# Moving the second batch's probability transposes from TensorE to VectorE and DMA

## The chip, the cores and the metric

One core of a Trainium2 chip runs the whole program. The metric is the device time of one execution in microseconds (us). The kernel was timed three times: median 715.22 us, lowest 714.57, highest 715.26.

## The reference

Causal attention of 4 batches, 12 heads, 448 positions and head size 64, and behind it a gated MLP over the 1,792 tokens (768 features, 1,536 hidden). Cut to what matters:

```python
scores = np.matmul(q, k.transpose(0, 1, 3, 2)) / np.sqrt(64)
scores = np.where(mask, -1e9, scores)            # mask: key later than query
attn = np.exp(scores - scores.max(-1, keepdims=True))
attn = attn / (attn.sum(-1, keepdims=True) + 1e-9)
x = np.matmul(attn, v)                            # then heads side by side: (1792, 768)
gate = 1.0 / (1.0 + np.exp(-(x @ w_gate)))
out = (gate * (x @ w_val)) @ w_out
```

The MLP's weights arrive as 8-byte numbers.

## The kernel before

**Units.** A batch is a unit. Its attention is done in six pairs of heads (`HP = 6`; pair `n` is `batch * 6 + k`), its MLP in 36 weight blocks of 128 by 768. Attention of batch 0 runs first by itself. Then the MLP of unit u runs on TensorE interleaved with the attention of batch u+1, u = 0 to 3; unit 3 has no attention beside it.

**MLP (L566 to L635).** Every product is made of three matmuls of 448 columns (high by high, high by low, low by high part), so a block is 18 matmuls on one stationary block of 128 by 128 each. `weight(p)` (L531) brings the block. In unit 0 each of the 36 blocks is loaded as 8-byte numbers into a part of the buffer `room` (L542, ring of three parts), ScalarE takes the high words (L545), three VectorE instructions assemble a 4-byte number (L547, L549, L552; tile `wr`, ring of three), and SyncE stores it to `wdram` (L555) for the later units, which only load it (L557). ScalarE then makes the high part `wh` (L560) and GpSimd the low part `wl` (L561), rings of three. So VectorE converts weights in unit 0 alone.

**Attention, narrow path (batches 0 and 1, `b < WIDE`).** Query blocks of 112 rows. `score` (L250): matmuls into the PSUM tiles `s`. `softmax` (L271): VectorE masks and takes the extreme (L279), ScalarE exponentiates (L283), VectorE adds 1e-9 and inverts once a pair (L290, L291), GpSimd scales (L302). `trans` (L304): 20 TensorE transposes in five groups into the PSUM tile `t`, each group emptied into `pt` by ScalarE or VectorE (L324, L326); `EV[1]` gives all five groups of batch 1 to ScalarE. `pv` (L328): 16 matmuls with `v` as the stationary operand and `pt` as the moving one. `features` (L345) splits the result into `xh` (ScalarE) and `xl` (VectorE).

**Attention, wide path (batches 2 and 3).** Query blocks of 128 rows, the last of 64 rows with both heads in one block. `wscore` (L366) and `wsoftmax` (L386) do the same work in other shapes (L396, L402), but add and invert three times a pair (L410, L412) and scale at L417. `shift` (L423) replaces the TensorE transposes: eight VectorE 32x32 transposes (L434, L437) write a buffer of 128 by 2048 named `tb`, and 16 DMAs of 64 KB (L443) issued by SyncE move its sixteen blocks of 32 partitions to their places in `pt`. `tb` is one of two halves of a stretch of `room`, which unit 0's weight loads use before. `wpv` (L447) makes 40 matmuls of 128 or 64 columns out of it.

**Order.** Nothing is ordered by hand. Each operation goes to `Plan.op` (L92) with its engine, a cost estimate, what it reads and writes, and sometimes a due time; a buffer that is used again waits for all operations of its former holder. `Plan.order` (L137) plays a list schedule: the engine that can start first takes, among its ready operations, the one with the earliest due time. The start times of that play fix the order of instructions on each engine, SyncE's queue of DMAs included, and each engine works strictly in that order:

```python
t = max(free[e], min(o.ready for o in q))
...
o = min((o for o in q if o.ready <= t + LOOK), key=lambda o: (o.due, o.n))
```

`att_steps` (L485) cuts a batch's attention into steps: at step m, scores of pair m, transposes of pair m-1, product with v of pair m-2 (`LAG = 1`). The main loop (L643) lets a step in each time its share of the attention falls behind the share of the MLP done, with the MLP's share divided by 0.9 in unit 0 and 0.98 later. A step of the wide path counts 1.0, one of the narrow path its estimated TensorE time.

Of the kernel before, what the change touches and what calls it, by code (L numbers as in the profile page):

```python
# [8 lines left out]
F32 = mybir.dt.float32  # L9
# [17 lines left out]
HP = H // 2  # L27

LAG = 1
WIDE = 2  # L30
WC = 512
EV = ((2,), (0, 1, 2, 3, 4), (1, 3, 4), (1, 3, 4))
BUFS = dict(w64=3, wd=2, wr=3, ws=3, sm=4, raw=3, pt=3, gt=5, vr=2, st=3)
LAT, LOOK, SLACK = 0.17, 0.06, 0.2


# [147 lines left out]
def kernel(  # L184
# [11 lines left out]
    def new(tag, shape, dtype, bufs=1, space=None):  # L196
        if tag not in pools:
            kw = {"space": space} if space else {}
            pools[tag] = ctx.enter_context(tc.tile_pool(name=tag, bufs=bufs, **kw))
        return plan.buf(pools[tag], bufs, shape, dtype, tag)  # L200
# [11 lines left out]

    room = new("room", [128, BUFS["w64"] * 2 * DM], F32)
    parts = []

    def part(n, k, i, both=False):

        old = parts[-BUFS["w64"]:] if both else parts[-k:-k + 1 or None]
        p = Part(room, i % k * n, n, Gone(old))
        parts.append(p)  # L220
        return p
# [17 lines left out]
    def load(n):  # L239
        j = pairs[n]  # L240
        j["raw"] = r = new("raw", [128, 2 * S], F32, BUFS["raw"])
        plan.op("SP", dma(128 * 2 * S * 4), lambda: nc.sync.dma_start(out=r.t, in_=qkt[n]), writes=[(r,)], extra=2.0)

    def load_v(n):
        j = pairs[n]
        j["vr"] = v = new("vr", [128, NB, 2, D], F32, BUFS["vr"])
        plan.op("SP", dma(128 * NB * 2 * D * 4), lambda: nc.sync.dma_start(
            out=v.t.rearrange("p c z d -> p (c z d)"), in_=vt[n]), writes=[(v,)], extra=2.0)

    def score(n, blocks, due):  # L250

        j = pairs[n]
        if blocks[0] == 0:
            j["sm"] = [new("sm", [128, SMW], F32, BUFS["sm"]) for z in range(2)]
            for k in ("mn", "sum", "r"):
                j[k] = new(k, [128, 2, NB], F32, BUFS["st"])
        r = j["raw"]
# [163 lines left out]
    shifted = []  # L421

    def shift(n):  # L423

        j = pairs[n]
        j["pt"] = pt = new("pt", [128, PTW], F32, BUFS["pt"])
        tb = part(4 * WC, 2, n, not shifted)
        shifted.append(tb)
        tv = lambda: tb.t.rearrange("p (r n) -> p r n", r=4)
        plan.op("PL", 0.2, lambda: nc.gpsimd.memset(tv()[:, 2:4, WC - 32:WC], 0.0), [], [(tb, "zero")])  # L430
        for z, i in [(z, i) for i in range(3) for z in range(2)] + [(0, 3)]:
            sm, o, c, at = j["sm"][z], woff(i), min(i + 1, 3), z * 192 + ioff(i) if i < 3 else 384
            r = [(sm, (i, z))] if i < 3 else [(sm, (i, 0), (i, 1))]
            plan.op("DVE", dve(128 * c) + 0.1, lambda sm=sm, i=i, o=o, c=c, at=at: nc.vector.transpose(  # L434
                out=tv()[:, :, at:at + 32 * c].rearrange("p r (c j) -> p c r j", j=32),
                in_=sm.t[:, o:o + 128 * c].rearrange("p (c r j) -> p c r j", r=4, j=32)), r, [(tb, (z, i))])
        plan.op("DVE", 0.2, lambda sm=j["sm"][0]: nc.vector.transpose(  # L437
            out=tv()[:, 0:2, WC - 32:WC],
            in_=sm.t[:, woff(3) + 384:woff(3) + 448].rearrange("p (r j) -> p r j", j=32)),
            [(j["sm"][0], (3, 0), (3, 1))], [(tb, "end")])  # L440
        for a in range(4):
            for r in range(4):
                plan.op("SP", 0.64, lambda a=a, r=r: nc.sync.dma_start(  # L443
                    out=pt.t[32 * r:32 * r + 32, a * WC:a * WC + WC], in_=tv()[32 * a:32 * a + 32, r]),
                    [(tb, "zero", "end", *[(z, i) for z in range(2) for i in range(3)], (0, 3))], [(pt, (a, r))], extra=2.0)
# [39 lines left out]
    def att_steps(b):  # L485

        L = []
        for m in range(HP + LAG + 1):
# [3 lines left out]
            if c is not None:  # L492
                L.append((0, lambda due, c=c: load_v(c)))
            if b >= WIDE:
                if c is not None:
                    L.append((0, lambda due, c=c: shift(c)))
                one, two = [], []
                if n is not None:
                    for bl, tag in ((0, 1), "s"), ((2,), "t"):
                        one.append((sum(keys(i) / 600 for i in bl) + 0.2, lambda due, n=n, bl=bl, tag=tag: wscore(n, bl, tag, due)))  # L500
                if d is not None:
                    two.append((2.0, lambda due, d=d: wpv(d, due)))
                if n is not None:
                    two.append((0.9, lambda due, n=n: wscore(n, (3,), "s", due)))
                for mine in (one, two):
                    if mine:
                        L.append((sum(w for w, _ in mine), lambda due, mine=mine: together(due, *(f for _, f in mine)), 1.0))
                    else:
                        L.append((0, lambda due: None, 1.0))
                continue  # L510
# [162 lines left out]
def _lay(q, k, v, moe_w_gate, moe_w_val, moe_w_out):  # L673
# [4 lines left out]
    vp = v.reshape(B * HP, 2, S, D)  # L678
    m = WIDE * HP
    vt[:m, :QB] = vp[:m].reshape(m, 2, NB, QB, D).transpose(0, 3, 2, 1, 4)  # L680
# [36 lines left out]
```

## Time and profile before

| | before |
|---|---|
| three timed runs, median (lowest to highest) | 715.22 us (714.57 to 715.26) |
| the profiled execution's own time | 714.69 us |
| its span, first to last instruction | 713.0 us |
| TensorE matmul busy | 688.6 us (97%) |
| VectorE busy | 315.3 us (44%) |
| ScalarE busy | 334.4 us (47%) |
| GpSimd busy | 435.0 us (61%) |
| mean granted TensorE clock | 0.988 of full speed |

The execution took 1.7 us more than its span. Busy time is the union of an engine's instruction times; matmuls are pipelined, so a busy TensorE is not one at its peak. The shares are means over stages that differ much: the first 66 us are the attention of batch 0, up to 258 us is unit 0 with the attention of batch 1, up to 418 us unit 1 with batch 2, up to 580 us unit 2 with batch 3, and then unit 3 by itself.

### The profile page before, as it was taken

What the parts mean: (1) busy time and instruction counts of PE and PEld (TensorE: products, weight loads), DVE (VectorE), ACT (ScalarE), POOL (GpSimd) and SP (SyncE); (2) the same over time, 40 slices, a digit from 0 to 9 for tenths busy, and PEclk for the clock granted to TensorE, in tenths of its full rate; (3) what the DMA queues carried; (4) which work ended last, traced back from release to release, by engine and by line L of the source; (5) the groups of instructions that cost most, each with busy time, mean ns of one, the idle gap of its engine ahead of it and who ended that gap; (6) DMA issues with size and microseconds to landing.
All of it is one profiled execution on the core that took longest, in us unless ns stands there. A gap on an engine that the chain in (4) does not pass through costs nothing.

```text
span 713.0 us, 11056 instructions
## 1 busy us (share of the span) xinstructions
PE 688.6 (97%) x3888; PEld 576.6 (81%) x3888; DVE 315.3 (44%) x784; ACT 334.4 (47%) x721; POOL 435.0 (61%) x388
## 2 busy tenths in 40 slices
PE   7989989899899899999999999999999999999997
PEld 4546767668688788888889988888889999999997
DVE  4898997788985324444541024444541000100000
ACT  6775546575565345543542245544552233333321
POOL 3472684858767456677665456677665456666652
PEclk9998999999899999999999999999999999999999
DMA  5484676676668435555466535555555433333341
GB/s 182 152 273 173 237 236 232 236 260 241 204 233 272 153 119 164 157 174 163 141 204 205 162 108 166 152 178 146 151 169 170 141 115 112 110 106 101 116 137 40
DMA packets 45559, 121.06 MB, mean 170 GB/s; under 512 B 7104, under 2 KB 10176, under 8 KB 45504
## 3 DMA queue, kind: packets, MB, share of 16 engines
q1 hardware_dynamic: 45504, 120.35, 52.8%
q8 instruction: 31, 0.51, 0.3%
q14 instruction: 24, 0.20, 0.1%
HBM read 88.08 MB, written 19.66 MB: 151 GB/s over the span
## 4 chain that ended last, share of the span: by engine, by line
PE 77%; DVE 8%; POOL 6%; issue 5%; ACT 3%; DMA 0%; DVEq 0%; POOLq 0%; ACTq 0%
PE m L577 64%; PE m L460 3%; PE s L381 3%; POOL wl L561 3%; POOL sm L302 3%; PE s L266 2%; DVE wr L549 2%; PE m L339 2%; DVE sm L279 2%; DVE wr L547 2%; PE t L315 1%; PE t L381 1%; DVE wr L552 1%; DVE pt L326 1%; ACT sm L283 1%
## 5 line engine op out<-in xcount | busy, mean ns | idle before, releaser
L561 POOL TENSOR_TENSOR wl<-wr,wh 128x768 fp32r<-128x768 f32 x144 | 271.9, 1888 | 215.3 <-ACT wh L560 200.5
L577 PE MATMUL m<-xh,wh 128*128 128x448 f32 x576 | 216.3, 375 | 3.2 <-DVE xl L348 3.2
L577 PE MATMUL m<-xl,wh 128*128 128x448 f32 x576 | 211.8, 368 | 0.0
L577 PE MATMUL m<-xh,wl 128*128 128x448 f32 x576 | 211.8, 368 | 0.0
L560 ACT CAST wh<-wr 128x768 fp32r<-128x768 f32 x144 | 120.2, 834 | 194.6 <-PE m L577 105.0
L577 PEld LDWEIGHTS m<-xh,wh 128*128 128x128 f32 x576 | 109.1, 189 | 27.7 <-issue 17.8
L577 PEld LDWEIGHTS m<-xh,wl 128*128 128x128 f32 x576 | 109.1, 189 | 9.1
L577 PEld LDWEIGHTS m<-xl,wh 128*128 128x128 f32 x576 | 109.3, 190 | 8.3
L577 PE MATMUL m<-gh,wh 128*128 128x448 f32 x288 | 106.6, 370 | 0.0
L577 PE MATMUL m<-gh,wl 128*128 128x448 f32 x288 | 105.2, 365 | 0.0
L577 PE MATMUL m<-gl,wh 128*128 128x448 f32 x288 | 105.2, 365 | 0.0
L604 DVE SCALAR_TENSOR_TENSOR gt<-gt,m 128x448 f32<-128x448 f32 x48 | 29.7, 618 | 130.8 <-PE m L577 106.7
L302 POOL TENSOR_SCALAR sm<-sm,r 112x112 f32<-112x112 f32 (+1 forms) x92 | 60.0, 669 | 37.1 <-DVE r L291 22.4
L402 ACT ACTIVATE sm<-sm,mn 128x128 f32<-128x128 f32 (+3 forms) x84 | 43.9, 525 | 44.3 <-DVE mn L396 44.3
L283 ACT ACTIVATE sm<-sm,mn 112x112 f32<-112x112 f32 (+2 forms) x96 | 50.0, 523 | 30.8 <-DVE mn L279 30.0
L607 POOL TENSOR_TENSOR gl<-gt,gh 128x448 fp32r<-128x448 f32 x48 | 62.3, 1297 | 2.3 <-ACT gh L606 2.3
L577 PEld LDWEIGHTS m<-gh,wh 128*128 128x128 f32 x288 | 54.1, 188 | 6.1 <-issue 1.4
L577 PEld LDWEIGHTS m<-gh,wl 128*128 128x128 f32 x288 | 54.1, 188 | 4.4
L577 PEld LDWEIGHTS m<-gl,wh 128*128 128x128 f32 x288 | 54.1, 188 | 4.1
L545 ACT ACTIVATE wd<-room 128x768 f32<-128x768 f32 x36 | 32.8, 912 | 49.3 <-DVE wr L552 24.4
L396 DVE CUSTOM_DVE_ANT_0 sm<-s,mask 128x128 f32<-128x128 f32 (+1 forms) x72 | 29.5, 443 | 59.7 <-PE s L381 59.1
L552 DVE SCALAR_TENSOR_TENSOR wr<-wd,wr 128x768 int32<-128x768 int32 x36 | 51.3, 1425 | 0.8
(45 smaller groups left out, 666.2 us busy)
## 6 DMA issues: line engine op xcount, KB each, us to landing
wr<-wdram SPq DMA_DIRECT2D x108, 384.0 KB, 3.1
room<-in_wp_dram SPq DMA_DIRECT2D x36, 768.0 KB, 5.3
wdram<-wr SPq DMA_DIRECT2D x36, 384.0 KB, 4.7
pt<-room SPq DMA_DIRECT2D x192, 64.0 KB, 2.5
raw<-in_qkt_dram SPq DMA_DIRECT2D x24, 448.0 KB, 4.3
vr<-in_vt_dram SPq DMA_DIRECT2D x24, 256.0 KB, 3.5
out_dram<-gt SPq DMA_DIRECT2D x24, 224.0 KB, 1.9
```

What stands on the lines that cost most here:

```text
L283: plan.op("ACT", act(ne, 0, 2), lambda z=z, sm=sm, i=i, ne=ne, off=off: nc.scalar.activation(out=sm.t[:QB, off:off + ne], in_=sm.t[:QB, of ...
L302: plan.op("PL", 0.35 + w / 1100, lambda args=args: nc.gpsimd.tensor_scalar(**args()), [(r_,)], [(sm, a)])
L381: nc.tensor.matmul(out=sp[z].t[place(z, i), o:o + ne], lhsT=r.t[h, s0:s0 + rows(i)], rhs=r.t[h, S:S + ne])
L396: plan.op("DVE", dve(ne) + 0.16, lambda z=z, y=y, sm=sm, i=i, o=o, ne=ne, off=off, s0=s0, at=at: nc.vector.tensor_tensor_reduce(out=sm.t[a ...
L402: plan.op("ACT", act(ne, 0, 2), lambda z=z, sm=sm, i=i, ne=ne, off=off: nc.scalar.activation(out=sm.t[:, off:off + ne], in_=sm.t[:, off:of ...
L545: plan.op("ACT", act(n) + 0.1, lambda: nc.scalar.activation(out=d.t.bitcast(F32), in_=hi().bitcast(F32), func=ACTF.Copy, scale=REBIAS), [( ...
L552: plan.op("DVE", 1.1, lambda: nc.vector.scalar_tensor_tensor(out=ri(), in0=d.t, scalar=-0x80000000, in1=ri(), op0=ALU.bitwise_and, op1=ALU ...
L560: plan.op("ACT", act(768), lambda: nc.scalar.copy(hi_.t, t.t), [(t,)], [(hi_,)])
L561: plan.op("PL", 1.87, lambda: nc.gpsimd.tensor_tensor(out=lo_.t, in0=t.t, in1=hi_.t.bitcast(F32), op=ALU.subtract), [(t,), (hi_,)], [(lo_,)])
L577: nc.tensor.matmul(out=ps.t[:, :S], lhsT=a.t[:, k, :], rhs=b.t if isinstance(b, Buf) else b(), start=(first and z == 0), stop=(last and z ...
L604: plan.op("DVE", dve(S), lambda: nc.vector.scalar_tensor_tensor(out=gg.t, in0=sg.t, scalar=1.0, in1=ps.t[:, :S], op0=ALU.add, op1=ALU.mult ...
L607: plan.op("PL", 1.3, lambda: nc.gpsimd.tensor_tensor(out=gl.t[:, jj], in0=gg.t, in1=gh.t.bitcast(F32), op=ALU.subtract), [(gg,), (gh,)], [ ...
```

## The change

Batch 1 takes the wide path too. Its VectorE transposes can't write into `room`, which unit 0's weight loads occupy, so they get a buffer of their own, `tb`, 128 by 2048 numbers, one copy. The ring of `pt` buffers goes from three to two. The host lays the rows of batch 1's `v` out in blocks of 128 in place of 112, since `_lay` goes by `WIDE`.

```diff
-WIDE = 2
+WIDE = 1
 WC = 512
 EV = ((2,), (0, 1, 2, 3, 4), (1, 3, 4), (1, 3, 4))
-BUFS = dict(w64=3, wd=2, wr=3, ws=3, sm=4, raw=3, pt=3, gt=5, vr=2, st=3)
+BUFS = dict(w64=3, wd=2, wr=3, ws=3, sm=4, raw=3, pt=2, gt=5, vr=2, st=3)
...
         j["pt"] = pt = new("pt", [128, PTW], F32, BUFS["pt"])
-        tb = part(4 * WC, 2, n, not shifted)
-        shifted.append(tb)
+        if n < 2 * HP:
+            tb = new("tb", [128, 4 * WC], F32)
+        else:
+            tb = part(4 * WC, 2, n, not shifted)
+            shifted.append(tb)
```

For batch 1 this puts `wscore`, `wsoftmax`, `shift` and `wpv` in the place of `score`, `softmax`, `trans` and `pv`, and its steps now count 1.0 each.

## Rows read from the trace of the kernel before

**Rows 1.** Busy time by stretch: us, then PE, PEld, DVE, ACT, POOL; PEclk, DMA share, GB/s

```profile
74.81:257.97 183.16, 171.36 (x907) 138.99 (x906) 135.07 (x199) 101.85 (x207) 121.17 (x93) 0.97 0.66 225
257.97:418.17 160.20, 160.20 (x986) 138.39 (x985) 56.58 (x198) 70.44 (x157) 100.59 (x96) 1.00 0.55 164
...
20.00:100.00 80.00, 74.06 (x437) 47.94 (x433) 73.18 (x169) 53.58 (x139) 45.59 (x54) 0.96 0.65 220
240.00:257.97 17.97, 17.97 (x91) 16.37 (x89) 0.23 (x1) 4.89 (x7) 8.35 (x5) 1.00 0.50 156
```

**Rows 2.** The same two stretches, the MLP's matmuls (L577) alone

```profile
74.81:257.97 183.16, 134.20 (x610) 0.97 0.66 225
257.97:418.17 160.20, 135.23 (x649) 1.00 0.55 164
```

**Rows 3.** Waits from 74.81 to 257.97 us: total us, times, longest

```profile
POOL wl L561 <- ACT wh L560: 47.0, 17, 5.8
DVE wr L547 <- POOL wl L561: 25.7, 13, 4.2
...
ACT wh L560 <- PE m L577: 14.7, 6, 4.4
...
PEld m L339 <- ACT pt L324: 6.6, 4, 3.5
```

**Rows 4.** VectorE's groups from 74.81 to 257.97 us: busy us, mean ns, idle before

```profile
L552 DVE SCALAR_TENSOR_TENSOR wr<-wd,wr 128x768 int32<-128x768 int32 x31 | 44.7, 1442 | 0.7
L549 DVE SCALAR_TENSOR_TENSOR wr<-room,wr 128x768 int32<-128x768 int32 x30 | 37.0, 1232 | 0.8
L547 DVE TENSOR_SCALAR wr<-wd 128x768 int32<-128x768 int32 x30 | 29.0, 965 | 25.7 <-POOL wl L561 25.7
...
L290 DVE TENSOR_SCALAR r<-sum 112x8 f32<-112x8 f32 x5 | 1.9, 381 | 1.4 <-ACT sm L283 1.2
L291 DVE RECIPROCAL r<-r 112x8 f32<-112x8 f32 x5 | 1.0, 203 | 0.2
```

**Rows 5.** Busy time of VectorE's L279 alone in the first stretch

```profile
74.81:257.97 183.16, 16.30 (x80) 0.97 0.66 225
```

**Rows 6.** Busy time of VectorE's L396 alone in the second stretch

```profile
257.97:418.17 160.20, 20.64 (x96) 1.00 0.55 164
```

**Rows 7.** VectorE's groups from 257.97 to 418.17 us

```profile
L434 DVE STREAM_TRANSPOSE room<-sm 128x384 f32<-128x384 f32 (+2 forms) x42 | 17.6, 446 | 16.9 <-POOL sm L417 11.9 <-DMA pt<-room 4.6
...
L410 DVE TENSOR_SCALAR r<-sum 128x4 f32<-128x4 f32 (+2 forms) x18 | 5.7, 335 | 10.2 <-ACT sm L402 9.9
...
L412 DVE RECIPROCAL r<-r 128x4 f32<-128x4 f32 (+2 forms) x18 | 2.7, 166 | 0.4
L437 DVE STREAM_TRANSPOSE room<-sm 128x64 f32<-128x64 f32 x6 | 1.3, 216 | 0.0
```

**Rows 8.** GpSimd's scaling in its groups, first stretch, then second

```profile
L302 POOL TENSOR_SCALAR sm<-sm,r 112x448 f32<-112x448 f32 (+3 forms) x45 | 33.9, 771 | 4.6 <-DVE r L291 4.6
...
L417 POOL TENSOR_SCALAR sm<-sm,r 128x256 f32<-128x256 f32 (+3 forms) x42 | 20.7, 506 | 3.6 <-DVE r L412 1.9 <-ACT sm L402 1.7
```

**Rows 9.** The conversion's lines, whole span: duration in ns, min/median/max, first and last start

```profile
L547 DVE TENSOR_SCALAR wr<-wd x36: 511/560/2247, 27.8 to 236.7; 128x768 int32<-128x768 int32 x36
...
L549 DVE SCALAR_TENSOR_TENSOR wr<-room,wr x36: 906/960/3358, 28.4 to 237.3; 128x768 int32<-128x768 int32 x36
...
L552 DVE SCALAR_TENSOR_TENSOR wr<-wd,wr x36: 907/978/3594, 33.6 to 238.3; 128x768 int32<-128x768 int32 x36
```

**Rows 10.** The page's costliest groups: low and high part of a block

```profile
L561 POOL TENSOR_TENSOR wl<-wr,wh 128x768 fp32r<-128x768 f32 x144 | 271.9, 1888 | 215.3 <-ACT wh L560 200.5
...
L560 ACT CAST wh<-wr 128x768 fp32r<-128x768 f32 x144 | 120.2, 834 | 194.6 <-PE m L577 105.0
```

**Rows 11.** The moves into pt (L443), whole span: ns on SyncE's queue, then time to landing

```profile
L443 SPq DMA_DIRECT2D pt<-room x192: 507/588/2105, 272.6 to 551.6; - x192
...
DMA to landing us min/median/max: 1.9/2.5/4.6
```

## The prediction

> **What bounds the kernel now.** I read the busy times by stretch first, then the waits of the stretch that changes, then VectorE's groups in it. The change lies in unit 0 with the attention of batch 1. The stretch from 74.81 us to the first scores of batch 2 at 257.97 takes 183.16 us; the like stretch of unit 1 with batch 2, already on the wide path, takes 160.20 [rows 1]. The reader is to see three differences. TensorE is never idle in the later stretch, and idle 183.16 - 171.36 = 11.8 us in the earlier one. The MLP's matmuls take 135.23 / 649 = 0.208 us each in the later and 134.20 / 610 = 0.220 in the earlier one [rows 2], at a mean granted clock of 0.97: some 7 us more over 610. And the attention itself takes 171.36 - 134.20 = 37.2 us of TensorE against 25.0.
>
> But VectorE is busy 135.07 us there and 56.58 in the later stretch, and it has nothing left after about 240: the last 18 us show 0.23 [rows 1]. Up to 240 it is busy 134.8 of 165.2 us, or 82%, and 25.7 us of its idle time wait for GpSimd to give a weight buffer back [rows 3]. GpSimd in turn waits for ScalarE, 47.0 us, and ScalarE partly for TensorE's matmuls, 14.7. So the conversion of weights and TensorE take turns in holding each other up: TensorE sets the end, some 18 us of matmuls behind VectorE, and VectorE is the next bound.
>
> **The change part by part.**
>
> *TensorE.* The earlier stretch lacks one pair's scores (done before it): 297 attention matmuls of the 312 of six pairs (16 scores, 20 transposes, 16 products each). At 37.2 / 297 = 0.125 us the missing 15 add 1.9: 39.0 us. The wide form takes 25.0. TensorE loses 14 us of work. The idle 11.8 and the slow 7 come from stalls such as products waiting for ScalarE's copies of `pt` (6.6) [rows 3], copies that go; that makes up to 33 us if VectorE could follow. ScalarE loses thirty copies and is busy 101.85 of 183, so I count nothing for it.
>
> *VectorE.* What goes is the narrow softmax. L279 is 16.30 us for 80 records [rows 5], 19.6 for 96. Sum and inverse are (1.9 + 1.0) x 6/5 = 3.5 [rows 4]. Together 23.1. No emptying goes, since batch 1's were all ScalarE's. What comes is 20.64 for L396 [rows 6], 17.6 + 1.3 for transposes and 5.7 + 2.7 for sums and inverses [rows 7]: 47.9. VectorE gains 24.8 us of work, on the engine that is next in line.
>
> *Relief on VectorE.* The conversion's lines have medians of 560, 960 and 978 ns, but single ones take up to 3,594 [rows 9], and their means in the stretch are 965, 1,232 and 1,442 [rows 4]. That is 30 x 0.405 + 30 x 0.272 + 31 x 0.464 = 34.7 us above the medians. I read it as waiting for GpSimd, busy 121 us there. GpSimd's scaling falls from 33.9 to about 20.7 us [rows 8], 13 of 121, so I allow 0 to 10% of 34.7, or 0 to 3.6 us. New VectorE work: 135.1 + 24.8 = 159.9 at most, 156.3 at least, 158.1 in the middle.
>
> *SyncE's queue.* 96 moves come into the stretch, each 0.588 us of the queue: 9.4 us a pair, 56 in all; a move lands 2.5 us after its issue [rows 11]. Behind them wait the weight loads (L542) and stores (L555), and behind those the conversion, three blocks deep. The moves end 9.4 + 2.5 = 12 us after a pair's last transpose. A pair comes each 160.20 / 6 = 27 us, so the single `tb` should be free again, and the product with v two steps later should find `pt` ready. Hidden, therefore, by that spacing; if it is not, each us that VectorE stands per pair costs 6.
>
> *DMA.* The rows give 0.66 x 183.16 = 121 us for 225 x 183.16 = 41.2 MB, 2.93 us a MB; in the later stretch 88.1 us for 26.3 MB. The moves are 96 x 64 KB = 6.3 MB. At the lower rate they cost 18 us, and 30 if the whole excess of the later stretch, 88.1 - 20.0 x 2.93, is theirs. So the 16 engines would be busy 139 to 151 us of some 180, up to 84%. I take that as no bound.
>
> The Trainium skill, "SBUF — State Buffer", section on door 1, the DMA port swizzle, speaks against the moves: a transfer over partitions 0 to 31 reaches 8 of 16 ports, so it has half the bandwidth. By it the moves would take 37 us (estimated as twice the 18 from the rows) and the total 158, some 88% of 180. The trace, with at most 30 us, stands under this. If the Trainium skill is right here, the DMA rival below gains.
>
> *`pt` two in place of three, and `tb`.* A pair's `pt` is written a whole step after the product of the pair two earlier was issued, on either path, so the third buffer's loss costs nothing unless attention runs ahead. If a pair did wait for the product before it, that would be one step.
>
> *The sum.* The nearest row to a bound by VectorE is 20 to 100 us, where it converts weights beside batch 0's and 1's attention: 73.18 of 80 us, 91.5% [rows 1]. 158.1 / 0.915 = 172.8 us from 74.81 puts its end at 247.6; with 156.3 and 159.9 it is 245.6 to 249.6. Behind the last conversion come the high part, 0.83, the low part, 1.89 [rows 10], and 18 matmuls of 0.208, 3.7: 6.5, with hand-overs 7. Unit 0 ends at 254.6 in place of 257.97, 3.4 us earlier. All after it is TensorE without a gap and stays. 714.69 - 3.4 = 711.3 for the profiled execution; that lies 0.53 under the median, so 711.8, say 712.0.
>
> The size hangs on that share: one point of it is 1.9 us, and 158.1 / (257.97 - 7 - 74.81) = 89.8% gives no gain at all. The measurement tells 0.2%, or 1.4 us, from no change.
>
> **The rivals.**
>
> *VectorE follows, TensorE stays the bound.* For it: apart from the 25.7 us, VectorE waits under 5 us in the stretch [rows 3, 4]. At 98% it ends 74.81 + 161.3 = 236.1, plus 7 is 243: 15 us earlier, 700. TensorE's own loss of 14 and part of its stalls allow it. Against it: 82% is what the stretch shows. Chance 0.12.
>
> *VectorE stands in its queue (slower).* Place: the first transposes of a pair wait for the one `tb`, whose moves stand in SyncE's queue between loads and stores that wait for VectorE's conversions. In the later stretch, with two halves and a slack VectorE, transposes already waited 16.9 us, 11.9 of it for GpSimd's scaling and 4.6 for moves [rows 7]. With conversions queued behind them such waits count. At 2 us a pair: 12 - 3.4 = 8.6 us later, 724. It decides from 3.4 / 6 = 0.6 us a pair. Against it: the order places conversions between. Chance 0.32.
>
> *DMA becomes the bound.* At the rows' upper end the DMA engines are busy 151 of 180 us, 84% where no stretch of the rows is over 66%; if weight loads then come late behind the moves, VectorE starves instead. Against it: at the lower end it is 77%. At 85% for VectorE the stretch ends 74.81 + 186 + 7 = 267.8, 10 us later, 725. Chance 0.07.
>
> *Nothing is won.* TensorE loses 14 us and stands 14 us more for weights; the share comes out within a point of 89.8%. 715. Chance 0.13.
>
> **How the numbers follow.** VectorE as the bound with 1.4 to 7 us gained has 0.36, and its own range is 708 to 714. Adding the rival at 700, faster has 0.48. The same has 0.13. Slower has 0.32 + 0.07 = 0.39. The range goes from 702, which leaves out half of the 700 case and little else, to 726, which leaves out the slower cases past 2.4 us a pair: about 2 in 10 together.
>
> **What would show it.** Right: in unit 0 VectorE's busy share rises from 82% to about 90%, its wait for GpSimd's weight buffers (L547) shrinks from 25.7 us to under 10, its busy time in unit 0 grows by 21 to 25 us, TensorE's idle time grows to about 20 us and now waits for weights (`wh` or `wl`) and no longer for `pt`; the stretch of unit 1 keeps its 160 us, with no idle TensorE. Wrong on the size: transposes waiting for moves or for L417 by several us a pair, or SyncE's moves followed by late loads. Wrong altogether: the stretch falls by 15 us or more with VectorE idle, or batch 0's attention grows for want of a third `pt`.

## The result, and the profile after

The changed kernel takes 721.81 us (median of 6 runs, 720.35 to 726.6) beside 714.55 us for the kernel before in the same comparison (6 runs, 713.24 to 715.26). The ratio is 1.0118, with a 95% interval of 1.0095 to 1.0141: it is slower by about 1.2%. The profiled execution took 720.35 us, its span 718.6 us, its mean granted clock was 0.974.

In the line numbers after, everything from `shift` on stands three lines lower: the moves L443 are L446, the conversion's three lines L547, L549, L552 are L550, L552, L555, the weight load L542 is L545, the store L555 is L558, the high and low parts are L563 and L564, the MLP's matmuls L580, the wide product with v L463.

The first part of the page of after gives busy time, share of the span and count for each engine:

```profile
PE 679.6 (95%) x3912; PEld 575.2 (80%) x3912; DVE 326.1 (45%) x856; ACT 319.6 (44%) x679; POOL 429.7 (60%) x388
```

TensorE works 9.0 us less than the 688.6 of before and stands idle for 718.6 - 679.6 = 39.0 us in place of 24.4. The difference, 14.6 - 9.0 = 5.6 us, is the whole change of the span. The first scores of batch 3 start at 423.80 us in place of 418.17 [rows 1], 5.6 us later too: all of it is lost before then.

Busy time by stretch in after, in the columns of [rows 1], with the stretch of unit 0 cut at 160 us and at the end of VectorE's last conversion, 254.61, and a row that starts at 74.81 us, where the prediction's sum starts:

```profile
64.76:160.00 95.24, 91.16 (x515) 75.82 (x514) 86.18 (x176) 53.57 (x114) 62.65 (x48) 0.96 0.68 227
160.00:254.61 94.61, 74.26 (x447) 63.00 (x448) 70.38 (x121) 38.17 (x67) 51.75 (x46) 0.89 0.76 255
64.76:259.36 194.60, 170.17 (x984) 142.95 (x983) 156.56 (x296) 93.79 (x185) 116.59 (x95) 0.93 0.72 243
259.36:423.80 164.44, 164.44 (x1007) 142.31 (x1006) 56.67 (x198) 71.86 (x158) 103.88 (x98) 1.00 0.57 173
74.81:254.61 179.80, 155.37 (x903) 130.81 (x902) 148.61 (x271) 85.15 (x164) 112.70 (x92) 0.93 0.72 240
```

The reader is to see four things. VectorE works 156.56 us in unit 0, but this stretch starts 10 us earlier than the one in [rows 1]; over the whole execution its work grew by 326.1 - 315.3 = 10.8 us only. It is busy 86.18 / 95.24 = 90.5% up to 160 us and 70.38 / 94.61 = 74.4% after it, 82.5% in all. TensorE is idle for 20.4 of the last 94.61 us, at a granted clock of 0.89. And unit 1's stretch is longer than the 160.20 us of before because 21 more matmuls fall into it (1,007 in place of 986); it has no gap and full clock, so the time is lost in unit 0.

What VectorE, TensorE and ScalarE wait for in unit 0 (line, total us, times, longest):

```profile
DVE r L410 <- ACT sm L402: 5.9, 3, 3.5
DVE xl L348 <- ACT xh L347: 5.9, 1, 5.9
DVE wr L550 <- DMA wdram<-wr: 5.5, 5, 4.0
...
DVE tb L437 <- DMA pt<-tb: 2.6, 1, 2.6
...
DVE wr L550 <- ACT wd L548: 1.8, 1, 1.8
...
PE m L463 <- DMA pt<-tb: 9.7, 3, 4.9
PE m L580 <- POOL wl L564: 5.5, 4, 1.9
PE m L580 <- ACT wh L563: 5.3, 2, 4.9
...
ACT wd L548 <- DMA room<-in_wp_dram: 21.4, 13, 3.7
```

The last of these in the kernel before:

```profile
ACT wd L545 <- DMA room<-in_wp_dram: 5.2, 4, 2.3
```

The 25.7 us for which the conversion waited for GpSimd [rows 3] are gone. About half of what came in their place leads to one queue: of the 33.3 us that VectorE stands from 64.76 to 254.61, 15.8 are waits for stores, for `wd`, for moves, and for `xl` behind the product (5.5 + 1.8 + 2.6 + 5.9). ScalarE, which makes `wd`, waits 21.4 us for weight loads in place of 5.2. SyncE's timeline shows why (start, duration, operation):

```profile
202.13 10.02 SPq L446 DMA_DIRECT2D pt<-tb  x16
212.19 0.58 SPq L558 DMA_DIRECT2D wdram<-wr  x1
212.88 0.39 SPq L545 DMA_DIRECT2D room<-in_wp_dram  x1
...
225.13 10.02 SPq L446 DMA_DIRECT2D pt<-tb  x16
235.25 0.53 SPq L545 DMA_DIRECT2D room<-in_wp_dram  x1
235.82 0.45 SPq L627 DMA_DIRECT2D out_dram<-gt  x1
236.32 0.43 SPq L558 DMA_DIRECT2D wdram<-wr  x1
```

The sixteen moves of a pair leave one behind the other and hold the queue for 10 us (all six pairs of batch 1 do so). Loads and stores of weights wait until the block is through, and then go out in a cluster. What that does to VectorE, on its own timeline of the same time (in brackets the idle time before, and its releaser):

```profile
232.49 0.96 DVE L555 SCALAR_TENSOR_TENSOR wr<-wd,wr 128x768 int32<-128x768 int32 x1
239.30 0.62 DVE L348 TENSOR_TENSOR xl<-m,xh 128x448 fp32r<-128x448 f32 x1 [5.85 <-ACT xh L347]
243.93 0.56 DVE L550 TENSOR_SCALAR wr<-wd 128x768 int32<-128x768 int32 x1 [4.01 <-DMA wdram<-wr]
```

In 10.5 us VectorE works 0.6. First it stands in front of `xl`, which follows the product with v, which follows the sixteenth move. Then it stands in front of a conversion whose buffer is free only when its store has landed, and that store waited in the queue behind the moves. The chain of waits tells the same (start, duration, what held it):

```profile
164.67 7.59 DMA wdram<-wr
172.35 1.45 DVE wr L550
...
189.50 6.78 DMA wdram<-wr
196.40 2.13 DVE wr L550
...
210.93 0.59 SPq L446
211.56 1.99 DMA pt<-tb
```

Twice a store that came late leads to the conversion (VectorE itself stood only 0.36 and 0.67 us for these two), and once the moves themselves, thirteen of which stand in the chain one after another ahead of the last landing.

### The profile page after: what moved, and what is told of

It reads as the page before. It is cut to its first block, busy times and chain, and to the rows that moved or that the text cites. A ratio compares the mean times of both kernels' runs of the same rounds, so it can differ in the third digit from the quotient of the medians.

```text
span 718.6 us, 11307 instructions
## 1 busy us (share of the span) xinstructions
PE 679.6 (95%) x3912; PEld 575.2 (80%) x3912; DVE 326.1 (45%) x856; ACT 319.6 (44%) x679; POOL 429.7 (60%) x388
## 4 chain that ended last, share of the span: by engine, by line
PE 75%; DVE 8%; issue 6%; POOL 3%; DMA 3%; ACT 2%; SPq 2%; POOLq 0%; DVEq 0%; ACTq 0%
PE m L580 62%; PE m L463 4%; PE s L381 4%; POOL wl L564 2%; SPq L446 2%; DMA wdram<-wr 2%; PE s L266 2%; DVE wr L550 2%; DVE wr L552 2%; PE t L381 1%; PE m L339 1%; DVE sm L279 1%; DVE wr L555 1%; DVE pt L326 1%; PE t L315 1%
## 5 line engine op out<-in xcount | busy, mean ns | idle before, releaser
L564 POOL TENSOR_TENSOR wl<-wr,wh 128x768 fp32r<-128x768 f32 x144 | 270.7, 1882 | 221.7 <-ACT wh L563 207.2
L580 PE MATMUL m<-xh,wh 128*128 128x448 f32 x576 | 214.2, 372 | 0.0
L580 PE MATMUL m<-xl,wh 128*128 128x448 f32 x576 | 210.4, 365 | 0.0
L580 PE MATMUL m<-xh,wl 128*128 128x448 f32 x576 | 210.4, 365 | 0.0
L563 ACT CAST wh<-wr 128x768 fp32r<-128x768 f32 x144 | 120.1, 835 | 200.1 <-PE m L580 94.2
L580 PEld LDWEIGHTS m<-xh,wh 128*128 128x128 f32 x576 | 108.2, 188 | 29.7 <-issue 17.2
L580 PEld LDWEIGHTS m<-xh,wl 128*128 128x128 f32 x576 | 108.2, 188 | 8.8
L580 PEld LDWEIGHTS m<-xl,wh 128*128 128x128 f32 x576 | 108.4, 188 | 8.2
L580 PE MATMUL m<-gh,wh 128*128 128x448 f32 x288 | 107.6, 374 | 5.3 <-ACT wh L563 5.3
L580 PE MATMUL m<-gh,wl 128*128 128x448 f32 x288 | 106.7, 371 | 5.5 <-POOL wl L564 5.5
L580 PE MATMUL m<-gl,wh 128*128 128x448 f32 x288 | 106.3, 369 | 0.0
L417 POOL TENSOR_SCALAR sm<-sm,r 128x384 f32<-128x384 f32 (+3 forms) x126 | 74.0, 602 | 27.9 <-DVE r L412 26.3
L607 DVE SCALAR_TENSOR_TENSOR gt<-gt,m 128x448 f32<-128x448 f32 x48 | 29.6, 617 | 133.2 <-PE m L580 112.8
L402 ACT ACTIVATE sm<-sm,mn 128x128 f32<-128x128 f32 (+3 forms) x126 | 65.8, 524 | 52.4 <-DVE mn L396 52.3
L396 DVE CUSTOM_DVE_ANT_0 sm<-s,mask 128x128 f32<-128x128 f32 (+1 forms) x108 | 44.5, 441 | 50.3 <-PE s L381 49.6
L580 PEld LDWEIGHTS m<-gh,wh 128*128 128x128 f32 x288 | 54.9, 191 | 12.7 <-ACT wh L563 6.2
L580 PEld LDWEIGHTS m<-gh,wl 128*128 128x128 f32 x288 | 54.8, 190 | 11.6 <-POOL wl L564 7.2
L610 POOL TENSOR_TENSOR gl<-gt,gh 128x448 fp32r<-128x448 f32 x48 | 58.8, 1225 | 2.4 <-ACT gh L609 2.3
L580 PEld LDWEIGHTS m<-gl,wh 128*128 128x128 f32 x288 | 54.9, 191 | 4.4 <-POOL gl L610 0.2
L463 PEld LDWEIGHTS m<-pt,vr 128*64 128x64 f32 x720 | 38.1, 151 | 19.4 <-issue 9.0
L463 PE MATMUL m<-pt,vr 128*64 128x128 f32 (+1 forms) x720 | 40.6, 274 | 13.7 <-DMA pt<-tb 9.7
L437 DVE STREAM_TRANSPOSE room<-sm 128x384 f32<-128x384 f32 (+2 forms) x84 | 35.2, 446 | 37.8 <-POOL sm L417 35.3
```

The source lines that it names most:

```text
L396: plan.op("DVE", dve(ne) + 0.16, lambda z=z, y=y, sm=sm, i=i, o=o, ne=ne, off=off, s0=s0, at=at: nc.vector.tensor_tensor_reduce(out=sm.t[a ...
L402: plan.op("ACT", act(ne, 0, 2), lambda z=z, sm=sm, i=i, ne=ne, off=off: nc.scalar.activation(out=sm.t[:, off:off + ne], in_=sm.t[:, off:of ...
L417: plan.op("PL", 0.35 + w / 1100, lambda sm=sm, i=i, o=o, w=w, z=z: nc.gpsimd.tensor_scalar(out=sm.t[:, o:o + w], in0=sm.t[:, o:o + w], sca ...
L463: nc.tensor.matmul(out=vp.t[64 * z:64 * z + 64, i * WQ:i * WQ + rows(i)], lhsT=v.t[:, c, z], rhs=src, start=(c == 0), stop=(c == i))
L563: plan.op("ACT", act(768), lambda: nc.scalar.copy(hi_.t, t.t), [(t,)], [(hi_,)])
L564: plan.op("PL", 1.87, lambda: nc.gpsimd.tensor_tensor(out=lo_.t, in0=t.t, in1=hi_.t.bitcast(F32), op=ALU.subtract), [(t,), (hi_,)], [(lo_,)])
```

## The experiments

Ratios are to the kernel before, run on the same chip beside it; differences between two changed kernels are differences of their ratios, times 714.55 us. The expectations name theories by letters. Q: the moves hold SyncE's queue, and the loads and stores behind them come late. V: VectorE has too much work. D: the DMA engines are full. P: the product with v waits for moves that end late. R: the shorter ring of `pt` costs time. O: the order that the planner makes.

**`pt` two in place of three, by itself** (the kernel before with this one edit).

```diff
-BUFS = dict(w64=3, wd=2, wr=3, ws=3, sm=4, raw=3, pt=3, gt=5, vr=2, st=3)
+BUFS = dict(w64=3, wd=2, wr=3, ws=3, sm=4, raw=3, pt=2, gt=5, vr=2, st=3)
```

> The kernel before with the pt ring of two in place of three, nothing else. Theory R (the shorter ring costs time in batch 0 or 1): 717 to 722 against 714.5. All others: 714 to 715.5.

714.53 us, ratio 1.001 (0.9995 to 1.0025). The ring costs nothing that can be told.

**One move in place of sixteen.** For batch 1 a single DMA of 1 MB carries the whole of `tb`.

```diff
-out=pt.t[32 * r:32 * r + 32, a * WC:a * WC + WC], in_=tv()[32 * a:32 * a + 32, r]),
+out=pt.t[32 * r:32 * r + 32, a * WC:a * WC + WC], in_=tv()[32 * a:32 * a + 32, r]) if n >= 2 * HP else
+nc.sync.dma_start(out=pt.t[:, :4 * WC], in_=tb.t) if (a, r) == (0, 0) else None,
```

> The changed kernel, but for batch 1 one DMA of 1 MB copies the transposed buffer straight to pt in place of the 16 moves of 64 KB; the blocks are not put in their places, so batch 1's probabilities are used in the wrong order. Bytes, order and all other work stay. Theory Q: SyncE is free 9 us a pair, time 706 to 711. Theory V and theory D: 720 to 722. Theory P: the product finds pt 7 us earlier, 716 to 719.

709.98 us, ratio 0.9943 (0.9923 to 0.9963). The same bytes move, VectorE's work is the same, and the kernel is 12.5 us (0.0175 x 714.55) faster than the changed one. Its stretches, again cut at 160 us and at the last conversion's end:

```profile
66.54:160.00 93.46, 90.20 (x528) 74.44 (x529) 85.85 (x174) 52.15 (x113) 61.40 (x48) 1.00 0.69 240
160.00:243.20 83.20, 72.78 (x442) 61.46 (x439) 71.04 (x122) 38.02 (x69) 57.23 (x46) 0.94 0.80 281
74.81:243.20 168.39, 154.71 (x915) 129.53 (x914) 149.50 (x272) 84.60 (x166) 118.04 (x92) 0.97 0.74 259
```

VectorE has 156.89 us of work again, but at a share of 88.8%, and ends at 243.20 in place of 254.61, 11.4 us earlier: from 74.81 us on it stands 168.39 - 149.50 = 18.9 us, where it stood 31.2. The move holds the queue for 0.47 us. ScalarE doesn't wait for a weight load any more, and TensorE waits for moves a single time, for 0.2 us. The forecast's 247.6 for VectorE's end and its time of 712.0 are what this kernel comes near to, not the changed one; in part by luck, since VectorE's work is 149.5 us here where the forecast had 158.1.

**One move, then fifteen idle ones.** Two things could have given that gain: the queue is free (theory Q), or the product no longer waits for a sixteenth move (theory P). Here the one move stands first, and in the places of the other fifteen stand DMAs of 16 KB into a buffer that nothing reads.

```diff
+nc.sync.dma_start(out=pt.t[:, :4 * WC], in_=tb.t) if (a, r) == (0, 0) else
+nc.sync.dma_start(out=scr.t[32 * r:32 * r + 32, 128 * a:128 * a + 128], in_=tv()[32 * a:32 * a + 32, r, :128]),
```

> As the run with one move of 1 MB for batch 1 (its blocks not put in their places), but with 15 small DMAs of 16 KB behind it into a buffer that nothing reads, in the queue places of the other moves. The product with v waits for the one move alone. Theory Q (SyncE's queue, held for 9 us a pair, makes the loads and stores behind it late): back to 719 to 722. Theory P (the 710 came from the product finding pt earlier): stays at 708 to 712.

726.66 us, ratio 1.0176 (1.0153 to 1.0199), 0.0233 x 714.55 = 16.6 us over the kernel with the one move. SyncE's timeline of this kernel:

```profile
157.72 0.52 SPq L451 DMA_DIRECT2D pt<-tb  x1
158.29 11.03 SPq L452 DMA_DIRECT2D scr<-tb  x15
169.36 0.58 SPq L563 DMA_DIRECT2D wdram<-wr  x1
```

And its waits in unit 0:

```profile
DVE wr L555 <- DMA wdram<-wr: 10.5, 6, 5.6
...
DVE tb L440 <- DMA scr<-tb: 5.3, 2, 3.6
```

No product waits for the fifteen, they carry a quarter of the bytes, and the loss is back, and more. So P alone does not give the gain. What the fifteen do is hold the queue, and `tb` with it: the conversion waits 10.5 us for its stores, ScalarE 33.5 us for weight loads, the transposes 5.3 us for `tb`. The order on SyncE and ScalarE is that of the changed kernel. Why it is worse than the sixteen real moves wasn't separated; 11.03 us are held in place of 10, and the time is above the 719 to 722 that theory Q gave.

**Less conversion**: the third conversion instruction runs over 64 of 768 columns, so that the other columns lack their sign. It is the test of how far VectorE's work is the bound; alone, and together with the one move.

```diff
-out=ri(), in0=d.t, scalar=-0x80000000, in1=ri(), op0=ALU.bitwise_and, op1=ALU.bitwise_or),
+out=ri()[:, :64], in0=d.t[:, :64], scalar=-0x80000000, in1=ri()[:, :64], op0=ALU.bitwise_and, op1=ALU.bitwise_or),
```

> The changed kernel, but the third assembling instruction of each weight block (L555) works on 64 of 768 columns, so the signs of the other columns are left out; order and all else stay. It takes some 36 x 1.1 = 40 us of work from VectorE. Theory V: the time falls by 20 us or more, to about 700. Theory Q: the stores and loads still stand behind the moves; only the first half of unit 0, where VectorE was 90% busy, can gain, so 714 to 720. Theory D: 718 to 722.

712.04 us, ratio 0.9968 (0.995 to 0.9987): 10.7 us (0.015 x 714.55) under the changed kernel. The instruction had taken 42.6 us in unit 0; its median fell from 0.96 to 0.23 us. The time lies under the 714 to 720 of theory Q and far above the 700 of theory V: neither was right alone.

> One move of 1 MB for batch 1 (blocks not put in their places) and the third assembling instruction on 64 of 768 columns (the other signs left out). Theory V with Q (with the queue free, VectorE's amount of work is the next bound): 40 us less work on VectorE gives 10 us or more, 690 to 700. If something else is the bound once the queue is free (rings, hand-overs, DMA engines): 706 to 711.

694.19 us, ratio 0.9704 (0.9681 to 0.9727). The one move gives 12.5 us alone, the smaller conversion 10.7 alone, and both together 0.0414 x 714.55 = 29.6, 6.4 more than their sum. With the queue free, less VectorE work is worth 17.1 us; with the queue held, 10.7. Up to 160 us TensorE is without a gap here:

```profile
65.74:160.00 94.26, 94.26 (x573) 78.50 (x573) 77.44 (x194) 56.69 (x125) 63.90 (x55) 1.00 0.77 267
```

So VectorE's work is the bound that lies under the queue, as the prediction had it. With both lessened the kernel is 0.0296 x 714.55 = 21.2 us under the one of before, of the 33 that the prediction gave as the most to be had from TensorE.

**Loads and stores of unit 0 by ScalarE's queue.** If SyncE's queue is the trouble, another queue for what waits behind it might help.

```diff
-lambda: nc.sync.dma_start(out=wd.t, in_=t.t)
+lambda: nc.scalar.dma_start(out=wd.t, in_=t.t)
```

(and the load L545 in the same way; the order was left as it was planned)

> The changed kernel, but unit 0's 36 weight loads and 36 stores (L545, L558) are issued by ScalarE's queue in place of SyncE's, in the same planned order. Theory Q (the 16 moves of a pair hold SyncE's queue for 10 us and the loads and stores behind them come late): VectorE's and TensorE's waits after 160 us go, the stretch of unit 0 falls from 194.6 to about 180 us, the time from 722 to 707 to 711. Theory V (VectorE simply has too much work) and theory D (the 16 DMA engines are full): 722 as before, since neither work nor bytes change. Theory P (the product with v waits for moves that end late): 719 to 722, since the moves themselves start no earlier.

740.32 us, ratio 1.0374 (1.0354 to 1.0393): a miss, outside every range given. I read it so: ScalarE works in order too, so a load whose buffer isn't free now holds up its casts and copies, and those hold up VectorE. The waits show the outcome and don't show that chain. The conversion waits 11.3 us for its stores though no move stands ahead of them, and in SyncE's queue the moves wait for transposes that come late:

```profile
SPq L446 <- DVE tb L440: 49.7, 4, 15.6
```

**Loads and stores ahead of the moves.** A key in the list schedule lets every other DMA that is ready go before batch 1's moves.

```diff
-key=lambda o: (o.due, o.n))
+key=lambda o: (o.late, o.due, o.n))
```

(`late` is 1 for batch 1's moves and 0 for all else)

> The changed kernel, but in the plan any load or store that is ready goes ahead of batch 1's moves in SyncE's queue. Theory Q: loads and stores now stand between the moves, VectorE no longer waits for them, and the time falls from 722 towards the 710 of the run with one move: 709 to 716. Theory P: the moves end later, so the product waits more: 722 to 728.

759.04 us, ratio 1.0635 (1.0596 to 1.0675): the worst of all. The sixteen moves are now spread over 25 us and more of SyncE's queue; its timeline shows the first of them, with loads and stores in the lines left out:

```profile
105.24 3.12 SPq L446 DMA_DIRECT2D pt<-tb  x5
...
111.91 0.52 SPq L446 DMA_DIRECT2D pt<-tb  x1
...
117.80 1.23 SPq L446 DMA_DIRECT2D pt<-tb  x2
...
131.65 3.40 SPq L446 DMA_DIRECT2D pt<-tb  x5
```

And the waits in unit 0, SyncE's own among them:

```profile
SPq L545 <- DVE wr L552: 50.5, 27, 3.0
SPq L558 <- DVE wr L555: 28.6, 21, 3.3
...
PE m L463 <- DMA pt<-tb: 50.1, 3, 23.4
...
DVE tb L437 <- DMA pt<-tb: 20.7, 3, 7.5
```

In the queue a load stands for the conversion that must free its buffer, 50.5 us, and a store for its own conversion, 28.6 us, and the moves stand behind both. The product waits 50.1 us for moves, and the transposes 20.7 us for the one `tb`. The rival "VectorE stands in its queue" described just this, and here it is; in the changed kernel its transposes stood only 2.6 us. (The waits of loads and stores are not what is new: in the kernel before they were 83.7 and 47.9 us, with no moves behind them in that unit.) Theory Q in the simple form that I had put, that it is enough to get the weights past the moves, falls, and the time is outside the ranges of both theories. Whoever stands second in this queue pays.

**The planner's costs set to what the queue shows.** The planner took a load or store for bytes / 355 GB/s + 0.03 us of the queue, so 2.2 us for a weight load of 768 KB, where the trace of the changed kernel has 0.33 to 0.60; a move it took for 0.64 us, near the 0.588 of the trace. Here every DMA but the moves is planned at 0.4 us of the queue with its landing behind; nothing else is changed, so only orders move. Once on the changed kernel, once on the kernel before.

```diff
-    dma = lambda b: b / 355e3 + 0.03
+    dma = lambda b: 0.4
+    land = lambda b: 2.0 + b / 355e3
```

> The changed kernel, but the planner counts 0.4 us of SyncE's queue for each load or store, as the trace has it, and puts the bytes in the latency (before, a load of 768 KB counted 2.2 us of the queue, so a pair of moves and the weights more than filled it in the plan). Only the order changes. Theory O (the moves stand in a block because the plan believes the queue full): loads and stores come between the moves, 708 to 716. If the block stays: 720 to 724.

> The kernel before with the same planner costs, to part the order's own gain from that of the wide path. Every theory: 710 to 716, since its queue was not full in the plan.

Changed kernel: 712.44 us, ratio 0.9989 (0.9978 to 1.0001), 0.0129 x 714.55 = 9.2 us under the changed kernel as it was. Kernel before: 714.62 us, ratio 1.0011 (0.9999 to 1.0023), no gain. I had expected the blocks of moves to be broken up. They were not, which should have left 720 to 724: they hold the queue for 10 us as before. But VectorE has other work in its order while they do, some of it batch 2's, drawn ahead of the last conversions. A block on SyncE's timeline of the changed kernel with these costs:

```profile
129.10 10.19 SPq L447 DMA_DIRECT2D pt<-tb  x16
```

Its stretch after 160 us:

```profile
160.00:250.00 90.00, 77.84 (x486) 64.80 (x485) 82.18 (x159) 45.51 (x96) 60.87 (x55) 0.94 0.79 269
```

Two of its waits in unit 0:

```profile
DVE wr L551 <- ACT wd L549: 1.5, 3, 0.7
...
PE m L464 <- DMA pt<-tb: 12.0, 3, 5.6
```

After 160 us VectorE is busy 91%, in place of 74.4%, and its conversion waits 1.5 us in all. TensorE still waits 12.0 us for moves. That fits a hold of the queue that costs as much as the orders of the other engines let it: a price where the next conversion in VectorE's order stands behind it, and little where it doesn't.

**Both orders together** (the two edits above):

> Planner costs as in the run with 0.4 us for each load or store, and loads and stores ahead of the moves as well. If what was left between 712.4 and 710 was the block of moves: 708 to 711. If it was VectorE's amount of work alone: 711 to 714. Theory P: 714 to 720.

741.9 us, ratio 1.0382 (1.0345 to 1.042), outside all three ranges. Better than `late` alone, and far worse than the costs alone; the product still waits 21.0 us for moves.

**Fewer DMAs by way of DRAM.** For batch 1 one store of 1 MB and four loads of 256 KB, each of 32 partitions, do what the sixteen moves did: five DMAs in place of sixteen, for twice the traffic.

```diff
+bd = new("bd", [128, 4 * WC], F32, 2, bass.MemoryType.DRAM)
+nc.sync.dma_start(out=bd.t, in_=tb.t)
...
+    out=pt.t[32 * r:32 * r + 32, :4 * WC].rearrange("p (a n) -> p a n", a=4),
+    in_=bd.t.rearrange("(a p) (r n) -> p a r n", a=4, r=4)[:, :, r]),
```

> The changed kernel, but batch 1's transposed buffer goes to DRAM in one store of 1 MB and comes back in four loads of 32 partitions, each block to its place: 5 DMAs a pair in place of 16, 12.6 MB of bytes in place of 6.3. Theory Q: the queue is held for 3 us a pair, 706 to 713. Theory D (the DMA engines are full): 722 or more. Theory P: the product finds pt about as late as now, 718 to 722.

712.81 us, ratio 0.9977 (0.9957 to 0.9997). Of the versions that compute the whole, this is the only one whose interval lies under the kernel before, by 0.2%. VectorE is now fed; the price is on the DMA engines, 93% busy after 160 us, and the product waits for its loads. Its stretch after 160 us, then one of its waits:

```profile
160.00:250.30 90.30, 78.11 (x482) 65.77 (x481) 85.26 (x137) 42.66 (x86) 57.34 (x47) 0.96 0.93 313
```

```profile
PE m L473 <- DMA pt<-bd: 8.4, 5, 2.9
```

**By way of DRAM, with the planner's costs** (both edits):

> The bounce through DRAM and the planner costs together. Theory Q: both shorten the hold of the queue, but together they can give no more than a free queue does, so at best about the 710 of the run with one move; 707 to 712. Theory V with Q (once the queue is free VectorE is the bound): the same 707 to 712, with VectorE busy over 88% up to its last conversion.

722.06 us, ratio 1.0094 (1.0066 to 1.0122), with runs from 715.51 to 725.49, where 707 to 712 was expected. The two gains don't add up: the DMA engines are busy 93% all the way from 100 to 240 us, and the product waits 19.4 us for its loads.

Not tried: two copies of `tb`, or a ring of three `pt` beside `tb`.

## Why the prediction was wrong

**The step that failed** is "SyncE's queue". It counted the moves rightly, 96 at 0.588 us, 9.4 us a pair, and 12 us to the last landing: the blocks take 10.0 us and a move lands 2.0 us after its issue. It then called them "hidden, therefore, by that spacing", since a pair comes each 27 us. That compares the block with the distance between pairs. What counts is the distance between what stands behind it: in unit 0 loads and stores for the conversion pass through the same queue every few microseconds, and the buffers of the conversion are two or three deep (`wd` two, `room` and `wr` three). A conversion takes some 3.5 us of VectorE (0.899 + 1.219 + 1.331, the means in this stretch), so three blocks of weights are used up in about 10 us if VectorE does nothing else. The row that the share was taken from, 91.5% over 20 to 100 us, was a stretch without moves. From 74.81 us to the last conversion the share measured 148.61 / 179.80 = 82.7%: VectorE stands 31.2 us where the sum had 172.8 - 158.1 = 14.7. It stood as long in the kernel before, 165.2 - 134.8 = 30.4; the wait for GpSimd went, and other waits, those of the queue foremost, took its place. With one move in place of sixteen VectorE stands 18.9 us, a share of 88.8%, and the kernel takes 709.98.

**A second error, which hid part of the first,** is the term "VectorE's work". It was to grow by 21.2 to 24.8 us and grew by 10.8. From 74.81 us on it is 148.61 us and not 158.1, 9.5 less, so the last conversion ends 7.0 us after the forecast's 247.6 and not 16.5. (156.56 us lies in the sum's 156.3 to 159.9 only because that stretch starts 10 us earlier.) What the narrow softmax took away was right, 23.5 us where 23.1 was named, and so was L396, 21.0 for 20.64. But transposes, sums and inverses take 22.1 us in place of 27.3, and the conversion's three lines take 121.4 us for all 36 blocks in place of 129.2, so 7.9 us less where 3.6 was the most allowed. The reason that I gave for that relief doesn't hold, since GpSimd's scaling stayed at 32.7 us in place of falling to 20.7; what did it stays open.

**What was right.** VectorE's work is the next bound once the queue is free. The ring of `pt`: no cost. The DMA engines: 72% busy in unit 0, under the 77 to 84% named, and not the cause, since the kernel with one move carries the same bytes in less time at a share of 0.80 after 160 us. Their busy time up to batch 2's first scores grew by some 14 us (0.69 x 259.36 - 0.64 x 257.97), where 18 to 30 were counted. The wait for GpSimd's buffers went from 25.7 us to nothing, where under 10 was named.

The Trainium skill's rule on ports ("SBUF — State Buffer", section on door 1, the DMA port swizzle) would by the prediction's estimate have added 37 us of DMA work here. The some 14 measured stand under it, so it didn't decide this case.

**Sizes that were off.** TensorE's work fell by 9.0 us, not by 14. Part of the rest is clock. Three of the six products of batch 1 in unit 0 were slow. Two rows of TensorE's timeline (start, duration, idle time before) and the same two stretches by window:

```profile
140.54 2.00 PE L463 MATMUL m<-pt,vr 128*64 128x128 f32 x40 [1.17 <-ACT gt L601]
164.83 3.68 PE L463 MATMUL m<-pt,vr 128*64 128x128 f32 x40 [4.92 <-DMA pt<-tb]
```

```profile
164.83:168.51 3.68, 3.68 (x42) 3.56 (x44) 3.30 (x7) 0.05 (x1) 3.68 (x6) 0.50 0.98 281
140.54:142.54 2.00, 2.00 (x42) 1.93 (x44) 2.00 (x8) 1.04 (x5) 0.02 (x1) 1.00 0.86 246
```

After an idle time of 4.92 us the granted clock was 0.50, the level of 1.2 GHz; after one of 1.17 us it was 1.00, 2.4 GHz. At 3.68, 3.68 and 3.30 in place of 2.00 us that is 4.7 us more of busy time. TensorE was to stand about 20 us in unit 0, for weights and no longer for `pt`; it stands 194.60 - 170.17 = 24.4, and 9.7 of it for `pt`.

**The rivals.** "VectorE stands in its queue (slower)" had the right place, SyncE's queue between loads and stores, and 724 us against 721.81 measured. That nearness is luck, for its mechanism was only a small part: transposes waited 2.6 us for moves. The greater parts were waits that it didn't name, the conversion for its own stores and loads (5.5 and 1.8 us), `xl` behind the product (5.9) and the product itself (9.7). "The DMA becomes the bound" was not so here; the version by way of DRAM, at 93%, came nearer to it.

What stays open: how the 7 us divide between VectorE's late conversions and TensorE's late product. Putting right the planner's costs took away the first and kept 12.0 us of the second, and won 9.2 us; but it changed the order of everything else as well.

## What to carry to other kernels

Count a queue of DMAs that one engine issues as an engine of its own: number of DMAs by the time that each holds it, and ask not whether a block fits between two blocks of its kind, but what else must pass in that time and how deep its buffers are. Letting either side go first only moves the wait; fewer issues, or an order that gives the waiting engine other work meanwhile, lessened it here. When a bound is lifted by a change, sum the next one in a stretch that already has the new traffic in it. And hold a forecast amount of work against one over the same work: two stretches that start at different points can agree by chance.

## What the runs showed of the hardware

- The time on SyncE's queue goes by the DMA and not by its bytes: 0.588 us for a move of 64 KB, 0.47 us for one of 1 MB inside SBUF, 11.03 us for fifteen of 16 KB (0.735 each), and 0.33 us for a weight load of 768 KB that finds the queue free.
- The Trainium skill ("DMA: Bandwidth & Descriptors", section "Issuing engines are not separate DMA queues") says that the time the sequencer takes to start a DMA is usually small beside the DMA itself. For one move the trace agrees, 0.588 us against 2.0 us to landing. For sixteen from one queue the issue times add up: 10.0 us of issue, and 2.0 us behind the last. The Trainium skill's rule to coalesce small transfers into one large one ("Rules for kernel authors") agrees with the kernel with one move, faster by 12.5 us.
- DMA engines can be 93% busy for 90 us while VectorE is 94% busy, in the version by way of DRAM; its loads of 256 KB then land in 6.7 us.
